# A fifth table from sums written four times, and a new written-out order of work, in an attention and ReGLU kernel on one core

## The chip, the core and the metric

The kernel runs on one NeuronCore of a Trainium2 chip. The metric is the device time of one execution in microseconds. The engines are named as in the profile: PE (TensorE, matmuls), PEld (its weight loads), DVE (VectorE), ACT (ScalarE), POOL (GpSimd) and SP (SyncE, here a queue that only issues transfers).

## The reference

Four batches of 12,416 tokens with 128 channels are attended to by 32 inducing points, the tokens then attend to the 32 results, and a gated feed-forward layer with 1,536 hidden units follows.

```python
def mab(q, kv):
    s = scale * (q @ kv.transpose(0, 2, 1))
    s = s - s.max(-1, keepdims=True)
    a = np.exp(s)
    a /= a.sum(-1, keepdims=True) + 1e-09
    return a @ kv
h = mab(I, x)                    # I: inducing points, (B, 32, 128)
x = mab(x, h).reshape(B * N, C)  # (49664, 128)
gate = np.maximum(x @ w_gate, 0.0)
val = x @ w_val
out = gate * val @ w_out
```

## The kernel before

**The idea.** After the second attention every token is a weighted mean of only 32 rows of h. The kernel takes the sign of each hidden unit's gate as one for the whole batch (it checks on the chip that this is certain, and falls back to a general kernel if it isn't). Gate times value is then a quadratic form in the 32 weights, and the output is a sum over pairs of rows: an exponential of a sum of two scores, times a table entry. The pairs are laid out as four full tables of 128 pairs, plus a fifth one with 16 sums in groups of 32 rows. The fifth stands four times, once for each row group, so that whichever row group a token block's exponentials `p` lie in finds its table.

**Stages.** The first batch's attention and tables are done ahead of everything (to about 40 us). What remains is interleaved by hand in the string `ORDER`, one letter for one step, and each letter takes the next step of its kind:

- `E` (`scores`): two matmuls of 512 columns make pair scores of 1,024 tokens' worth of columns (`e_ps`, two buffers), and ACT takes their exponential into `F` (20 buffers).
- `O` (`outputs`): five matmuls of 129 columns for one tile of 128 tokens, four with `F` and `T`, one with `p` and the fifth table. After three tiles DVE takes the reciprocal of the denominators (`rzo`) and multiplies into `osb`; after six tiles SP's queue stores `osb` (four buffers). There are 97 tiles in each batch, 388 in all.
- `s` (`pair_scores`, `pair_copy`, `pair_reach`): four matmuls into column groups, then two DVE passes. Some `s` steps are the bound on the error (`bound1` to `certain`) and the last is the flag for the fallback.
- `x` (`pair_exp`): ACT's exponential of single scores, `p`.
- `p` (`plan_phase1`): the next batch's first attention: for batch 1 six steps of eight PE transposes, then score and sums for each chunk of 16 tiles, the end of h (`h_end1`, `h_end2`), the gates (`gates`, four steps), their sums and signs, and the masks (`masked`).
- `u`: the products of gates and values (`products`), their joins, the fifth table's sums (`fifth`), and the tables (`table`, `table5`). A batch's tables must stand in `T` before its first `O`.
- `l` and `t`: a load of a chunk of x by POOL's queue, and its DMA transpose on SP's queue, which the stores use as well. A `t` takes the chunk that was loaded last.

All engines run in order, so `ORDER` sets which step waits behind which on each of them.

**Names that the change touches.** `lhs5` holds the fifth table's sums, the weights of its matmuls; half of each group of 32 is zero. `fifth(b, 0)` makes the first product `u16`, `fifth(b, 1)` the second product and the sum. `table5(b)` multiplies them with `wo` (for batch 0 with the masked copy `won`) for each of 12 groups of hidden units, into the four row groups of one bank, and DVE copies the bank to `T` with a mask (`quarter`).

Of the kernel before, what the change touches and what calls it, by code (L numbers as in the profile page):

```python
# [11 lines left out]
FP16 = mybir.dt.float16  # L12
AF = mybir.ActivationFunctionType
ALU = mybir.AluOpType
# [3 lines left out]
def quadratic_kernel(tc, x, inducing, moe_w_gate, moe_w_val, moe_w_out, out):  # L18


    with ExitStack() as ctx:
        return quadratic_body(
            ctx, tc, x, inducing, moe_w_gate, moe_w_val, moe_w_out, out
        )


def quadratic_body(ctx, tc, x, inducing, moe_w_gate, moe_w_val, moe_w_out, out):
    nc = tc.nc
    B, N, C = x.shape
    M = inducing.shape[0]  # L30
    DFF = moe_w_gate.shape[1]
    P = 128
# [4 lines left out]
    NFF = DFF // P  # L37
# [6 lines left out]
    H = M // 2  # L44
# [8 lines left out]
    def st(shape, dtype, tag, bufs, name=None, pool=None):  # L53
        return (pool or sb).tile(shape, dtype, tag=tag, bufs=bufs, name=name or tag)
# [8 lines left out]
    wo = constp.tile([P, NFF, P], FP16, name="wo")  # L63
# [47 lines left out]
    mp = ctx.enter_context(tc.tile_pool(name="mp", bufs=1))  # L111

    def mt(shape, dtype, tag, bufs, name=None):
        return st(shape, dtype, tag, bufs, name, pool=mp)
# [1 line left out]
    ga, gb, va, vb = (mp.tile([P, NFF, M + NS], FP16, name=n) for n in ("ga", "gb", "va", "vb"))  # L116
    U = [mp.tile([P, NFF, NS, M], FP16, name=f"U{i}") for i in range(2)]
    won = mp.tile([P, NFF, P], FP16, name="won")
    lhs5 = mp.tile([P, NFF, M], FP16, name="lhs5")


    def windows(out, h):
# [201 lines left out]
    with tc.tile_pool(name="sp", bufs=1) as sp, tc.tile_pool(  # L324
        name="psum0", bufs=1, space=bass.MemoryType.PSUM
# [5 lines left out]
    def bank(tag, name, shape, dtype=FP32):  # L331
        return psum.tile(shape, dtype, tag=tag, bufs=2, name=name)
# [8 lines left out]
    dve, act, pool = nc.vector, nc.scalar, nc.gpsimd  # L341
# [182 lines left out]
    def fifth(b, k):  # L524

        s = state[b]
        if k == 0:
            s["u16"] = mt([P, NFF, H], FP16, "u16", 1)
            dve.tensor_tensor(out=s["u16"], in0=ga[:, :, 0:H], in1=va[:, :, H:M], op=ALU.mult)
            return  # L530
        u = lhs5[:, :, 0:H]
        dve.tensor_tensor(out=u, in0=ga[:, :, H:M], in1=va[:, :, 0:H], op=ALU.mult)
        dve.tensor_tensor(out=u, in0=u, in1=s["u16"], op=ALU.add)

    def table5(b):
        ps = bank("m", "T5_ps", [P, P])
        for t in range(NFF):
            for r in range(4):
                nc.tensor.matmul(  # L539
                    ps[32 * r : 32 * r + 32, :],  # L540
                    lhs5[:, t, :],
                    (wo if b else won)[:, t, :],
                    start=t == 0,
                    stop=t == NFF - 1,
                )
        dve.tensor_tensor(
            out=T[b % 2][:, 4:8, 0:P],
            in0=ps.unsqueeze(1).broadcast_to([P, 4, P]),
            in1=quarter.unsqueeze(2).broadcast_to([P, 4, P]),
            op=ALU.mult,  # L550
        )
# [121 lines left out]
    def plan_phase1(b):  # L673
# [120 lines left out]
        for j in range(4):  # L794
            for odd in range(2):
                for i in range(2):
                    todo.append(f(products, i, 0, NFF, 4 * j, 4 * j + 4, odd))
            todo.append(f(joined, j))
            late.append((len(todo) + 1, f(table, b, j)))
            if j == 1:  # L800
                todo += [f(fifth, b, 0), f(fifth, b, 1)]
                late.append((len(todo) + 1, f(table5, b)))
# [51 lines left out]
    pair_exp(0, 0)  # L854
    all_k(7, 4)
    fifth(0, 0)
    fifth(0, 1)
    table_all(0, 7, 4)
    all_k(11, 1)
    table5(0)  # L860
    table_all(0, 11, 1)
    scores(0, 0, 1, 0)
# [12 lines left out]
    for step in ORDER:  # L875
        if step == "E":
            scores(*next(units))
        elif step == "O":
            b, t = next(tiles)
# [8 lines left out]


ORDER = (  # L890
    "EOpOsExOpOEEpOOOEOOEppOEuEpOOOpEEspOOxOOpOllEElsplOOpOEEOlOOOppEEpOppOpEsEpOpOOEEpOOpEpE"
    "OOOxOsEEOOOpOpEOOpOpOtEpEOpOOEOOpOtEOEtOEuOuOOuxtOOEtusEOuOuEOOOEuuOOxEsuuEuOOOEslsOEOuu"
    "OsuluEEOpOOOEEuOEpEuOpOEEuuuOOxuOOuEEssOOOxOEEpOpuOOOtEuuEupOOtpOEEOuOOOEEOppOOOEEsOOOOl"
    "OlxEEOOpxOOOEEOlOOlOpOEEspxOOOOEEOlOOOpOEEOOOpEOEppOOEEOOpOtpEEpOOpOOOOEEOOtpOOpOEOEOOpO"
    "EsExOOOtutOEEuOOOutOEOuussEOEOOOExuuuOOEElsOOOupluuOEsEsOOEOuxOuEEpuOpEuEuOuOxOOEEOuOOOu"
    "uEOOEsuEuOOEEtuOOpEOuOupOEuEOOtOpEsEOOpuEEsOOOOOEEOOOxOpsEEOOOOpOOEEpOpOOOxOEEspOOpOEOpE"
    "OEppEOOEOOppOEOppOOEpEOOOpOOEOOEpOxOOuOEEuOOOsEOuOOuusEOEOuEOOuEEuuOOOEOOOEsuEOxuOOOEEus"
    "sOOuExuOOOxuEEsuEOuOEOOuEOOEOOOxEuEuOuOOOOEsEuOuOEEOOOOOuEEuuOOOOOEEOuOsEEOOOEOOOxOOOEEO"
    "OOOOOEEOOxOOOOEEOOOOOOEEOOOOOxOEEOOOOOOEEsOOxOOOEEOOOOOsEEOOOOOsEEOOOOsOOEEOOOOOOEEOsOOE"
    "OEOOOxsOOEEOOOOOEsOEOOOxOEEOOOOOOOOOOOO"  # L900
)


# [202 lines left out]
```

## Time and profile before

| | |
|---|---|
| time, median of three | 273.76 us (273.37 to 273.79) |
| span of the profiled execution | 273.0 us |
| mean granted clock of TensorE | 0.984 |
| PE busy | 253.8 us |
| ACT busy | 228.4 us |
| DVE busy | 214.2 us |
| first output tile, last output tile | 40.7 us, 266.3 us |
| DMA transpose on SP's queue, median of issuing one | 3.1 us |

Busy shares are averages over the span. In what follows, "stretch" is the time between two output tiles of the loop. A row of the costliest groups gives the line in the kernel, the engine, the operation, what is written from what, the shape and the number of instructions; then the busy time, the mean of one in ns, and the idle time of the engine just before them with what ended it. A matmul's end is modelled and includes its latency, so how many fit in a time is read from the starts of the steps that follow each other.

### The profile page before, as it was taken

To read this page: it belongs to the slowest core of one execution; us is meant where nothing else is said; L and a number is where in the kernel's file an instruction comes from. 1 tells how busy PE (TensorE), PEld (TensorE's weight loads), DVE (VectorE), ACT (ScalarE), POOL (GpSimd) and SP (SyncE) were. 2 spreads that over 40 slices of the span, in tenths; PEclk is the share of its full clock that TensorE was granted. 3 is DMA by queue.
4 is the path that set the end of the run, shared out by engine and by line. 5 is a ranking of instruction groups with operands and counts; after the bars stand their busy time and mean duration, and the time that the engine had idled before them with its cause. 6 is when DMAs were issued, how large, how long until landed. Compare 5 with 4: busy or idle time off the path is not lost.

```text
span 273.0 us, 9520 instructions
## 1 busy us (share of the span) xinstructions
PE 253.8 (93%) x4029; PEld 189.2 (69%) x4029; DVE 214.2 (78%) x583; ACT 228.4 (84%) x305; POOL 27.2 (10%) x71
## 2 busy tenths in 40 slices
PE   2998699999999999999899999999899999999990
PEld 0786587776666777776667777767677777878770
DVE  4565958866999997766899998778999997678651
ACT  4133689999999999999799999999899988988940
POOL 8372000210000200400002000000010000000000
PEclk9999599999999999999999999999999999999998
DMA  7999988999499889899999989331421333443333
GB/s 178 201 208 204 214 170 104 249 199 243 168 209 178 209 226 220 208 224 271 232 217 228 176 241 204 118 119 60 166 116 70 118 118 138 163 175 149 144 140 113
DMA packets 48738, 48.38 MB, mean 177 GB/s; under 512 B 35472, under 2 KB 36656, under 8 KB 48688
## 3 DMA queue, kind: packets, MB, share of 16 engines
q1 hardware_dynamic: 41520, 33.74, 43.8%
q0 software_dynamic: 6880, 13.50, 27.8%
q8 instruction: 33, 0.54, 0.8%
q10 hardware_dynamic: 288, 0.46, 0.5%
q14 instruction: 17, 0.14, 0.2%
HBM read 27.80 MB, written 25.43 MB: 195 GB/s over the span
## 4 chain that ended last, share of the span: by engine, by line
PE 79%; DVE 9%; ACT 7%; issue 3%; POOL 0%; ACTq 0%; DVEq 0%; POOLq 0%
PE o_ps L591 32%; PE e_ps L569 16%; PE o_ps L593 7%; ACT F L576 5%; PE T_ps L519 3%; PE T_ps L505 3%; PE s_ps L707 3%; PE s_ps L372 3%; DVE osb L608 2%; PE xT_ps L262 2%; PE hz_ps L729 2%; PE s_ps L273 1%; PE hz_ps L720 1%; PE T_ps L539 1%; PE xT_ps L698 1%
## 5 line engine op out<-in xcount | busy, mean ns | idle before, releaser
L576 ACT ACTIVATE F<-e_ps 128x1024 f16<-128x1024 f32 x192 | 185.6, 1026 | 15.4 <-PE e_ps L569 13.0
L591 PE MATMUL o_ps<-T,F 128*128 128x129 f16 x1536 | 129.4, 221 | 1.9 <-DVE osb L608 1.0
L591 PEld LDWEIGHTS <-F 128*128 128x128 f16 x1536 | 98.5, 97 | 28.1 <-issue 19.7
L593 PE MATMUL o_ps<-T,p 128*128 128x129 f16 x388 | 84.5, 218 | 0.0
L608 DVE TENSOR_TENSOR osb<-o_ps,rzo 128x384 f32<-128x384 f32 x132 | 72.5, 549 | 4.8 <-DVE rzo L607 0.2
L569 PE MATMUL e_ps<-sc,sel 32*128 32x512 f16 x384 | 60.0, 385 | 0.5 <-ACT F L576 0.3
L593 PEld LDWEIGHTS <-p 128*128 128x128 f16 x388 | 37.9, 98 | 0.4
L607 DVE RECIPROCAL rzo<-o_ps 128x3 f32<-128x3 f32 x132 | 23.0, 174 | 18.7 <-PE o_ps L593 17.4
L569 PEld LDWEIGHTS <-sel 32*128 32x128 f16 x384 | 16.1, 91 | 18.1 <-issue 5.4
L628 DVE TENSOR_SCALAR sc<-s_ps 128x512 f16<-128x512 f32 (+1 forms) x28 | 17.6, 627 | 2.8 <-PE s_ps L372 2.3
L640 DVE TENSOR_REDUCE reach<-sc 128x1 f32<-128x512 f16 (+1 forms) x28 | 17.5, 627 | 1.0
L655 ACT ACTIVATE p<-sc 128x512 f16<-128x512 f16 (+1 forms) x28 | 16.3, 584 | 0.0
L275 ACT ACTIVATE p<-s_ps 128x256 f16<-128x256 f32 (+3 forms) x16 | 5.3, 332 | 12.2 <-PE s_ps L273 12.2
L263 DVE COPY xT<-xT_ps 128x1024 f16<-128x1024 f16 (+2 forms) x15 | 8.8, 583 | 5.8 <-PE xT_ps L262 4.4
L709 ACT ACTIVATE p<-s_ps 128x512 f16<-128x512 f32 (+1 forms) x21 | 11.4, 547 | 0.7 <-PE s_ps L707 0.7
L442 POOL TENSOR_SCALAR ok<-eps 128x1 f32<-128x1 f32 x4 | 1.1, 285 | 100.6 <-DVE eps L403 100.6
L482 DVE TENSOR_TENSOR U<-U,U 128x1536 f16<-128x1536 f16 (+1 forms) x12 | 10.9, 906 | 0.4
L505 PE MATMUL T_ps<-won,U 128*128 128x128 f16 x96 | 8.3, 262 | 2.4 <-DVE U L473 2.4
L505 PEld LDWEIGHTS <-U 128*128 128x128 f16 x96 | 7.5, 121 | 4.0 <-DVE U L473 3.9
L519 PE MATMUL T_ps<-wo,U 128*128 128x128 f16 x144 | 10.1, 219 | 0.0
L707 PE MATMUL s_ps<-indT,xT 128*128 128x32 f16 x288 | 10.0, 177 | 0.0
L86 POOL DMA_DIRECT2D x<-in_x_dram x18 | 9.7, 551 | 1.7 <-PE s_ps L273 1.2
(159 smaller groups left out, 255.2 us busy)
## 6 DMA issues: line engine op xcount, KB each, us to landing
out_dram<-osb SPq DMA_DIRECT2D x64, 384.0 KB, 2.8
x<-in_x_dram POOLq DMA_DIRECT2D x18, 512.0 KB, 11.7
x<-in_x_dram POOLq DMA_DIRECT2D x8, 256.0 KB, 8.0
x<-in_x_dram POOLq DMA_DIRECT2D x5, 128.0 KB, 8.1
osb<-in_x_dram ACTq DMA_DIRECT2D x1, 384.0 KB, 4.5
osb<-in_x_dram SPq DMA_DIRECT2D x1, 384.0 KB, 4.4
wg<-in_moe_w_gate_dram POOLq DMA_DIRECT2D x1, 384.0 KB, 8.1
wv<-in_moe_w_val_dram POOLq DMA_DIRECT2D x1, 384.0 KB, 8.7
```

Of the source, the lines that this page charges most:

```text
L505: nc.tensor.matmul(s["T_ps"][j // 2][:, j % 2, :], u_cols(i, t, j), won[:, t, :], start=False, stop=(i, t, j % 2) == (1, NFF - 1, 1),)
L519: nc.tensor.matmul(ps, u_cols(0, t, j), wo[:, t, :], start=t == 0, stop=t == NFF - 1)
L569: nc.tensor.matmul(ps[:, r, :], sel4[rows, j, :], sc[rows, :], start=True, stop=True)
L576: act.activation(out=F[b, q, d, j], in_=ps, func=AF.Exp, scale=sm_scale2)
L591: nc.tensor.matmul(ps, f, T[b % 2][:, j, 0 : P + 1], start=j == 0, stop=False)
L593: nc.tensor.matmul(ps, p2s[b, q][rows, tok], T[b % 2][rows, 4 + r, 0 : P + 1], start=False, stop=True)
L607: dve.reciprocal(out=rz[:, 0:k, :], in_=outputs.ps[:, 0:k, P : P + 1])
L608: dve.tensor_tensor(out=osb[:, a6 : a6 + k, :], in0=outputs.ps[:, 0:k, 0:P], in1=rz[:, 0:k, :].broadcast_to([P, k, P]), op=ALU.mult,)
L628: dve.tensor_scalar(out=scs[b, q][0:k, 0:w], in0=ps[0:k, 0:w], scalar1=64.0, scalar2=-64.0, op0=ALU.min, op1=ALU.max,)
L640: dve.tensor_reduce(out=state[b]["reach"][0:k, q : q + 1], in_=scs[b, q][0:k, 0:w], axis=AX.X, op=ALU.max, apply_absolute_value=True,)
L655: act.activation(out=p2s[b, q][0:k, 0:w], in_=scs[b, q][0:k, 0:w], func=AF.Exp, scale=sm_scale2)
L707: nc.tensor.matmul(ps[:, t, :], s["xT"][q][:, t, :], indT, start=True, stop=True)
```

## The change

Two things change. First, the sums of the fifth table are written four times side by side into a larger `lhs5`, so that 12 matmuls with 128 weight columns fill all four row groups at once; before, 48 matmuls of 32 weight columns each filled one row group. The product goes into a buffer of its own rather than into `lhs5`. Second, `ORDER` is replaced by another string with the same number of each letter (191 E, 388 O, 82 u, 75 p, 40 s, 27 x, 14 l, 14 t). It was searched for with the stores on SyncE's queue, which both kernels use.

```diff
-    lhs5 = mp.tile([P, NFF, M], FP16, name="lhs5")
+    lhs5 = mp.tile([P, NFF, 4, M], FP16, name="lhs5")
...
-            s["u16"] = mt([P, NFF, H], FP16, "u16", 1)
+            s["u16"] = mt([P, NFF, H], FP16, "u16", 2)
             dve.tensor_tensor(out=s["u16"], in0=ga[:, :, 0:H], in1=va[:, :, H:M], op=ALU.mult)
             return
-        u = lhs5[:, :, 0:H]
+        u = mt([P, NFF, H], FP16, "u16", 2)
         dve.tensor_tensor(out=u, in0=ga[:, :, H:M], in1=va[:, :, 0:H], op=ALU.mult)
-        dve.tensor_tensor(out=u, in0=u, in1=s["u16"], op=ALU.add)
+        u, u16 = (v.unsqueeze(2).broadcast_to([P, NFF, 4, H]) for v in (u, s["u16"]))
+        dve.tensor_tensor(out=lhs5[:, :, :, 0:H], in0=u, in1=u16, op=ALU.add)
...
         for t in range(NFF):
-            for r in range(4):
-                nc.tensor.matmul(
-                    ps[32 * r : 32 * r + 32, :],
-                    lhs5[:, t, :],
-                    (wo if b else won)[:, t, :],
-                    start=t == 0,
-                    stop=t == NFF - 1,
-                )
+            nc.tensor.matmul(
+                ps,
+                lhs5[:, t, :, :].rearrange("p r m -> p (r m)"),
+                (wo if b else won)[:, t, :],
+                start=t == 0,
+                stop=t == NFF - 1,
+            )
```

The start and the end of the two strings (the rest differs in the same manner):

```diff
 ORDER = (
-    "EOpOsExOpOEEpOOOEOOEppOEuEpOOOpEEspOOxOOpOllEElsplOOpOEEOlOOOppEEpOppOpEsEpOpOOEEpOOpEpE"
+    "pEsEOOOOOxEEpOpOEpEOEOsEpOOxEEOOOppOEEsplOOpOxEEpsOOlpOOEEuOOlOpOOpEEppOOEppOOEEpsllOlpO"
...
-    "OEOOOxsOOEEOOOOOEsOEOOOxOEEOOOOOOOOOOOO"
+    "OOEEOOOOOsxEEOOOOOOEEOOOOEOOEOOOOOOOOOO"
 )
```

Where the steps of the later batches fall, by the output tile after which they come:

| step | before | after |
|---|---|---|
| loads of batch 2 | 17, 17, 17, 17, 21, 66, 69 | 14, 19, 23, 30, 30, 31, 34 |
| transposes of batch 2 | 43, 49, 50, 54, 56, 88, 90 | 53, 61, 61, 61, 62, 65, 73 |
| score steps of batch 2 | 70, 75, 85, 90, 96, 113, 122 | 72, 76, 78, 85, 88, 93, 95 |
| gates of batch 2 | 131, 132, 132, 134 | 111, 114, 115, 120 |
| products of batch 2, first and last | 150, 187 | 133, 188 |
| transposes of batch 3 | 132, 140, 150, 150, 154, 183, 190 | 113, 118, 125, 129, 156, 164, 171 |
| gates of batch 3 | 222, 222, 224, 224 | 197, 199, 205, 210 |
| products of batch 3, first and last | 236, 283 | 224, 281 |

More of the change, by code (lines that the diff above doesn't have):

```diff
@@ L890 @@
 ORDER = (
-    "EOpOsExOpOEEpOOOEOOEppOEuEpOOOpEEspOOxOOpOllEElsplOOpOEEOlOOOppEEpOppOpEsEpOpOOEEpOOpEpE"
[L892 to L899, printed above, removed]
-    "OEOOOxsOOEEOOOOOEsOEOOOxOEEOOOOOOOOOOOO"
+    "pEsEOOOOOxEEpOpOEpEOEOsEpOOxEEOOOppOEEsplOOpOxEEpsOOlpOOEEuOOlOpOOpEEppOOEppOOEEpsllOlpO"
+    "EEpOEppOlOEOOEpOpOOEEsOOpOOEsOOOpEEspOpOOEOEOOpEtOOxuOOEEOuOOOttuEtOsutEuOuOEOtEOsEOuOxO"
+    "uEuuEOOOpOutuEEOOEpsEOuupEuEOuuupEOxpEOxuuOOOpsEEOuOOpuuOEuEpOOupOxOEEslpOuOOpOEEllpOupO"
+    "EEOpOxOOlOEEpOOOpEOOEOOEsEOOOpOEEOtOpOpOOOtEEOOpOOOEEOOtpOOOEpOtEpOOOOsuxEEOpuOOOOEuEpul"
+    "lOOlpOEEsOuOOOEpuEOOxOuusEuEpuOOuOOOEEusOOOuEEptxuOusOOOOEEsuEOOEsOEEtOuOOEOOOpxOEtEsxpO"
+    "OOOuOEEOOuuOOpOEEspOOOuEEOOpuEEOuOuuOpuEOpOOEEOpupxEEOOpOOEpOOpOOEEOOOOpOsEEOOOOpOEpEOOO"
+    "OpEOOEpOOOxOEEOOOuuOEOOEusEOOEOuOEOOEuxOOuOOEEOuOOuuOEEuOOOuxOOOuEEOOOususEEOOxOOOOEEsOO"
+    "OuEssuxEEOOOOEuxOOEEuOOuOEOOuOsEEOOOuuEuEOOOOuEOOEOEuOOEOuxOOsEEOOOOuEEsOOOOEEOOOOOEEOOO"
+    "OOOxEEOOOOEOOEOOOOxEEOOOOOEsEOOOOEEsOOEOOOEOOOOEEOOOOOsEEOOxOOOOEEOOOOOOEEOsxOOOOsEEOsOO"
+    "OOEEOOOOOsxEEOOOOOOEEOOOOEOOEOOOOOOOOOO"
 )
```

## The prediction

> **What bounds the kernel now.** I read four views: busy shares, costliest groups, the chain that ended last, and busy time by stretch. First the shares:
>
> ```profile
> PE 253.8 (93%) x4029; PEld 189.2 (69%) x4029; DVE 214.2 (78%) x583; ACT 228.4 (84%) x305; POOL 27.2 (10%) x71
> ```
>
> PE looks like the bound, but its ends are modelled, so 93% can't be read as peak. The chain is needed as well:
>
> ```profile
> PE 79%; DVE 9%; ACT 7%; issue 3%; POOL 0%; ACTq 0%; DVEq 0%; POOLq 0%
> PE o_ps L591 32%; PE e_ps L569 16%; PE o_ps L593 7%; ACT F L576 5%; PE T_ps L519 3%; PE T_ps L505 3%; PE s_ps L707 3%; PE s_ps L372 3%; DVE osb L608 2%; PE xT_ps L262 2%; PE hz_ps L729 2%; PE s_ps L273 1%; PE hz_ps L720 1%; PE T_ps L539 1%; PE xT_ps L698 1%
> ```
>
> Most of the chain is PE, yet it passes to ACT and DVE for whole stretches. The group rows say why:
>
> ```profile
> L576 ACT ACTIVATE F<-e_ps 128x1024 f16<-128x1024 f32 x192 | 185.6, 1026 | 15.4 <-PE e_ps L569 13.0
> L608 DVE TENSOR_TENSOR osb<-o_ps,rzo 128x384 f32<-128x384 f32 x132 | 72.5, 549 | 4.8 <-DVE rzo L607 0.2
> ```
>
> Now the busy time by stretch, cut at every 24th output tile (columns: window, then busy us and instructions of PE, PEld, DVE, ACT, POOL; clock; DMA):
>
> ```profile
> 57.50:75.30 17.80, 17.39 (x319) 12.57 (x317) 13.64 (x41) 16.52 (x24) 0.00 (x0) 1.00 0.83 215
> 75.30:90.30 15.00, 14.96 (x196) 10.35 (x194) 14.41 (x42) 13.85 (x18) 0.00 (x0) 1.00 1.09 194
> 120.20:134.40 14.20, 12.93 (x211) 9.93 (x208) 9.73 (x33) 12.69 (x18) 0.00 (x0) 1.00 1.02 253
> 148.60:166.50 17.90, 17.82 (x331) 12.98 (x329) 17.05 (x43) 17.48 (x24) 1.85 (x6) 1.00 0.97 222
> 194.20:210.50 16.30, 15.96 (x239) 11.29 (x236) 15.29 (x45) 15.43 (x21) 1.47 (x3) 1.00 0.32 123
> 222.60:234.00 11.40, 11.40 (x161) 8.69 (x159) 8.56 (x23) 10.22 (x14) 0.00 (x0) 1.00 0.35 133
> ```
>
> From the first output tile (40.7 us) to the last exponential (262.7) ACT is busy 208.8 of 222 us, DVE 186.4. Three engines are nearly full and take turns: DVE in tiles 48-72 and 240-264 (14.4 of 15.0, 15.3 of 16.3), ACT in 168-192 (17.5 of 17.9), while in 222.6:234.0 DVE works 75% of the time. So ORDER, which says what stands beside what, sets the end.
>
> **The skill.** Perfetto Trace Analysis, Identifying the Most-Contended Engine: matmul busy time is a poor measure of how near TensorE is to its limit. The trace agrees: a single 128-column matmul shows 219 ns, while 12 in a row (L519) take 0.67 us. TensorEngine Tiling (Array Packing), Key Properties: different array tiles work in parallel; Restrictions there: column tiling turns fast weight load off. VectorE: DVE Perf Modes, the perf-mode tier table: a 16-bit tensor_tensor runs at up to two elements a cycle; the trace's 128x1536 fp16 add at 906 ns and 128x768 multiply at 549 ns give 0.46 ns per further element, which agrees.
>
> **Part 1, fifth table on PE.** Removed: 48 matmuls of 32 columns per batch (192 in all). Added: 12 of 128. The chain prices both:
>
> ```profile
> 149.82 0.80 PE T_ps L519 x12
> 153.03 0.84 PE T_ps L539 x48
> 206.12 0.67 PE T_ps L519 x12
> 208.96 0.67 PE T_ps L539 x48
> ```
>
> Four column groups already run side by side, so 48 small ones take about what 12 full ones take, not four times as much. From the first matmul of a table to the next step's start I read 0.67-0.78 us for L519 and 0.79-0.80 for L539. Saving: 4 x 0.11 = 0.4 us of PE, of which the three in the loop count only where PE is the bound: 0.1 to 0.4, I take 0.2.
>
> **Part 2, sums written four times (DVE).** Before, per batch: 248 + 248 + 259 ns. The last one now writes 128x768 through a broadcast. The nearest row is L473's fp16 multiply with a broadcast input, 128x768, 549 ns; without the double rate the elements would take 768/384 times what L608's f32 elements take, about 1.1 us. I take 0.55: +0.29 us x 4 = 1.2 us of DVE (at most 3.4). Batch 0's stands ahead of the last products of the opening, which ended at 36.2 us while PE used them after 39.3; three us hide it. The others lie in DVE-heavy stretches, so 0.3-0.6 us may show. The second u16 buffer costs nothing and takes a write-after-read wait away. The zeroing of lhs5 on POOL grows from 384 to 1536 elements (0.46 us before; 0.9 more at the most pessimistic linear rate) and delays the loads of batch 1, issued from 18.6 us. Their first reader on PE comes at 40.9 and the first loads landed at 29.3: hidden.
>
> **Part 3, ORDER.** The letters are the same in number; only places change. Price per step, as what it adds to its engine's busy time (PE: usual distance to the next step's start): E 0.27 PE, 0.95 ACT; O 0.29 PE, 0.25 DVE; x 0.47 ACT; s 0.33 PE, 1.22 DVE; score 0.40 PE, 0.47 ACT; sums 0.51 PE, 0.22 DVE; PE transpose 0.45 PE, 0.63 DVE; gates 0.15 PE, 0.30 ACT, 0.41 DVE; h_end2 1.96, gate sums 1.09, masks 1.33, a product 0.45, a join 0.90 DVE; table 0.68 PE, 0.19 ACT. Summed over each stretch of 24 tiles, the fullest engine has (us):
>
> before: 16.6, 16.7, 16.9, 17.3, 12.1, 12.2, 17.1, 17.8, 13.9, 13.4, 17.0, 11.7, 11.6, 9.4, 10.2, 9.1, last four tiles 1.2; sum 224.4.
> after: 18.0, 17.2, 14.0, 20.6, 12.8, 13.5, 15.7, 13.9, 13.3, 11.7, 13.8, 13.0, 10.7, 10.3, 9.6, 9.4, 1.2; sum 218.7.
>
> The first sum is near the measured 225.6 us (40.7 to 266.3), so the count is usable. It falls by 5.7. Why: the new order starts batch 2's gates at tile 111 rather than 131 and its products at 133 rather than 150, batch 3's gates at 197 rather than 222 and its products at 224 rather than 236. The DVE-heavy stretches (16.9, 17.1, 17.0) drop to 14.0, 15.4, 13.8 on DVE, and that work lies where PE and ACT have enough to do too. The crowd in the chain at 128-140 us (gates, sums, masks, then outputs, all DVE) should thin out.
>
> But exponentials run ahead through buffers, so stretches aren't hard walls, and another cut gives another number: falls of 2.6 (24 tiles, shifted by 12), 3.7 and 1.2 (32), 2.1 and 3.9 (48), 4.1 and 6.8 (16), 3.4 and 2.5 (12). The mean of these nine is 3.4; I take that.
>
> Ends: a PE transpose now stands before the first O, where PE waited 0.42 us for T: 0.3 gained. Against it, the SyncE queue. Batch 2's five large transposes now stand together at tiles 61-65, after one at 53. Each occupies that queue 3.1 us (median), so the store of tiles 60-65 leaves about 12 us after the group starts at some 85 us, near 97, landing by 100-102 (stores beside loads and transposes took 2 to 9 us). Its osb buffer is wanted again at tile 84, some 99-101 us in the new order. DVE's eviction of tile 84 may wait 0-2 us there, and behind it in DVE's queue stand joins and copies, then PE for an o_ps bank. I take 0.5. The transposes themselves land by 90, 93, 96, 99 and 103, their score steps come at about 95, 97, 102, 104 and 109: no wait. Loads for batch 2 all go out by tile 34, 19 tiles ahead of the first transpose that needs them; before, two went out at 66 and 69.
>
> The tail: before, PE stood 0.7 us before tile 379 for the last full exponential, which ACT had begun only after the matmuls of the small last unit, 0.38 us later than it could. The new order issues that unit two tiles later, so I estimate 0.2 gained.
>
> Sum: -3.4 (balance) -0.2 (table on PE) +0.5 (wider add, where DVE is full) -0.3 (first O) +0.5 (store wait) -0.2 (tail) = -3.1. 273.8 - 3.1 = 270.7.
>
> **Rivals.** (a) The load count holds in full: 5.7 us of balance, near 268; for it, the 24-tile cut reproduces before best. (b) Short waits, not stretch loads, set the pace: ACT's 13 us of idle come in gaps under 0.8 us, each from the local place of E among O's, and a new order makes its own. Then the gain is 0 to 1.5 us, 272.3-273.8. (c) Slower: transposes in a row hold stores back as above, DVE waits on osb two or three times, 2 us each, and the fourth stretch (20.6 us on PE, 18.8 DVE, 19.6 ACT: all three full, no slack for waits) runs over by 1-2 us; with the gain of 3.4 eaten by these, 274.5-277. Against (c): before, stores took up to 10.1 us to land on the same queue, and no DVE wait for one shows.
>
> **How the numbers follow.** Forecast, gain 1.5-4.7 us: 0.53. (a): 0.13. (b): 0.16, of which 0.06 falls within 0.2% (273.2-274.3) and 0.10 is faster. (c): 0.18. Faster 0.76, same 0.06, slower 0.18. Range: (a) with the largest fall read, 6.8, reaches 266.8; upward, half of (c): 275.2.
>
> **What would show it.** Right: DVE-led chain pieces at 128-140 and 185-194 us shrink; ACT idle after 40 us falls below 11 us; L539 shows 48 matmuls of 128 columns, 0.68 us per table; the last add is 0.5-0.6 us. Wrong: DVE evictions released by a store's DMA near tile 84, scores waiting for a transpose, or ACT idle as long as before with the same balance of loads.

## The result, and the profile after

| | before | after |
|---|---|---|
| time, median of four | 273.77 us (273.37 to 274.42) | 271.88 us (271.49 to 272.28) |
| ratio, 95% interval | | 0.9929 [0.9903, 0.9954] |
| first PE step of ORDER to last output tile | 225.8 us | 224.0 us |
| tile 0 to tile 360 | 213.8 us | 209.6 us |
| tile 360 to the last one, 387 | 11.7 us | 12.9 us |

The change makes the kernel 1.9 us faster; the forecast was 3.1. The third row is the interleaved part alone. It is the one to compare: the opening before it differs from run to run (the first step came at 40.1 us before and at 39.4 us after), while the loop's stretches repeat to about 0.03 us in traces of the same order. One exception bears on this table. In the trace of the kernel before, tiles 24 to 48 take 17.8 us, and in experiments 1, 10 and 11, which have the same order there, 17.4. So some 0.4 us of the 225.8 belong to this one execution and not to its order, and the loop's own fall is about 1.4 us. In the fourth row 1.2 us of the fall are not a gain: the new order does three more PE steps ahead of its first output tile. From the first PE step to tile 360 the fall is 3.0 us (2.6 without those 0.4), and the last row then gives 1.2 back.

The page's busy shares after (the kernel before had 253.8, 189.2, 214.2 and 228.4 us):

```profile
PE 250.4 (93%) x3885; PEld 187.1 (69%) x3885; DVE 214.6 (79%) x583; ACT 228.5 (84%) x305; POOL 27.8 (10%) x70
```

DVE and ACT do nearly the same work as before. Of PE's 144 fewer matmuls nothing can be read in busy time, since their ends are modelled. The chain after, shares by engine and by line:

```profile
PE 69%; DVE 11%; ACT 7%; DMA 6%; issue 4%; POOL 0%; ACTq 0%; DVEq 0%; POOLq 0%
PE o_ps L591 29%; PE e_ps L569 15%; PE o_ps L593 6%; DMA x<-in_x_dram 6%; ACT F L576 6%; DVE osb L608 4%; PE T_ps L505 3%; PE T_ps L519 3%; PE s_ps L707 3%; PE s_ps L372 3%; PE hz_ps L729 2%; DVE U L473 1%; PE xT_ps L698 1%; PE T_ps L539 1%; PE hz_ps L720 1%
```

The 6% of DMA is in the opening, where in this run the loads of x came last. In the loop the chain is still PE's steps with pieces of ACT and DVE; DVE's share has grown from 9% to 11%. The two large groups, by line:

```profile
L576 ACT ACTIVATE F<-e_ps 128x1024 f16<-128x1024 f32 x192 | 185.1, 1026 | 13.1 <-PE e_ps L569 10.8
L608 DVE TENSOR_TENSOR osb<-o_ps,rzo 128x384 f32<-128x384 f32 x132 | 72.5, 549 | 4.5
```

ACT's idle time before exponentials fell from 15.4 to 13.1 us: some waits have gone, far from all. The same stretches of output tiles that the prediction showed, now with the times at which the new kernel reaches them, to about 0.4 us (window, then busy us and instructions of PE, PEld, DVE, ACT, POOL; clock; DMA):

```profile
57.90:75.80 17.90, 17.53 (x319) 12.70 (x317) 12.57 (x43) 17.15 (x24) 0.53 (x1) 1.00 1.05 256
75.80:89.30 13.50, 12.78 (x166) 8.86 (x164) 12.86 (x35) 12.73 (x17) 0.88 (x3) 1.00 0.94 195
122.40:135.10 12.70, 11.98 (x206) 9.22 (x204) 11.99 (x32) 11.63 (x15) 1.22 (x3) 1.00 1.02 248
151.40:165.40 14.00, 14.00 (x256) 10.80 (x253) 13.39 (x32) 13.62 (x20) 0.00 (x0) 1.00 0.76 202
192.00:205.30 13.30, 13.19 (x181) 9.91 (x179) 11.92 (x37) 12.98 (x18) 0.61 (x3) 1.00 0.33 131
218.30:229.90 11.60, 11.60 (x159) 8.60 (x157) 8.32 (x22) 10.81 (x14) 0.00 (x0) 1.00 0.32 121
```

Tiles 240-264 (fifth line) took 16.3 us before and take 13.3 now. But the work went elsewhere, as the elapsed time of all stretches shows (us, from the start of one tile to that of the tile 24 later):

```
tiles from   0    24    48    72    96   120   144   168   192   216   240   264   288   312   336   360
before    16.9  17.8  15.1  17.3  12.6  14.1  14.2  18.0  13.7  13.9  16.3  12.1  11.4   9.8  10.6  10.7
after     16.6  18.0  13.4  20.8  12.3  12.7  16.3  14.0  14.3  12.3  13.3  13.0  11.6  10.9  10.0  11.9
```

Single stretches move by up to 4 us, while their sum falls by 3.0. The last three hold no work of later batches in either order: 312-336 loses 1.1 us, with one `E` more than before, 336-360 wins 0.6, and 360-384, with as many `E` as before, loses 1.2.

### The profile page after: what moved, and what is told of

It reads as the page before. It is cut to its first block, busy times and chain, and to the rows that moved or that the text cites. A ratio compares the mean times of both kernels' runs of the same rounds, so it can differ in the third digit from the quotient of the medians.

```text
span 270.5 us, 9238 instructions
## 1 busy us (share of the span) xinstructions
PE 250.4 (93%) x3885; PEld 187.1 (69%) x3885; DVE 214.6 (79%) x583; ACT 228.5 (84%) x305; POOL 27.8 (10%) x70
## 4 chain that ended last, share of the span: by engine, by line
PE 69%; DVE 11%; ACT 7%; DMA 6%; issue 4%; POOL 0%; ACTq 0%; DVEq 0%; POOLq 0%
PE o_ps L591 29%; PE e_ps L569 15%; PE o_ps L593 6%; DMA x<-in_x_dram 6%; ACT F L576 6%; DVE osb L608 4%; PE T_ps L505 3%; PE T_ps L519 3%; PE s_ps L707 3%; PE s_ps L372 3%; PE hz_ps L729 2%; DVE U L473 1%; PE xT_ps L698 1%; PE T_ps L539 1%; PE hz_ps L720 1%
## 5 line engine op out<-in xcount | busy, mean ns | idle before, releaser
L576 ACT ACTIVATE F<-e_ps 128x1024 f16<-128x1024 f32 x192 | 185.1, 1026 | 13.1 <-PE e_ps L569 10.8
L591 PE MATMUL o_ps<-T,F 128*128 128x129 f16 x1536 | 128.5, 221 | 2.5 <-DVE osb L608 2.1
L591 PEld LDWEIGHTS <-F 128*128 128x128 f16 x1536 | 98.6, 97 | 27.8 <-issue 19.6
L608 DVE TENSOR_TENSOR osb<-o_ps,rzo 128x384 f32<-128x384 f32 x132 | 72.5, 549 | 4.5
L569 PE MATMUL e_ps<-sc,sel 32*128 32x512 f16 x384 | 59.0, 385 | 0.2
L607 DVE RECIPROCAL rzo<-o_ps 128x3 f32<-128x3 f32 x132 | 23.0, 174 | 17.3 <-PE o_ps L593 15.6
L569 PEld LDWEIGHTS <-sel 32*128 32x128 f16 x384 | 15.2, 91 | 17.8 <-issue 5.8
L275 ACT ACTIVATE p<-s_ps 128x256 f16<-128x256 f32 (+3 forms) x16 | 5.3, 332 | 11.9 <-PE s_ps L273 11.9
L709 ACT ACTIVATE p<-s_ps 128x512 f16<-128x512 f32 (+1 forms) x21 | 11.5, 550 | 0.7 <-PE s_ps L707 0.5
## 6 DMA issues: line engine op xcount, KB each, us to landing
x<-in_x_dram POOLq DMA_DIRECT2D x18, 512.0 KB, 11.9
```

Of the source, the lines that this page charges most:

```text
L569: nc.tensor.matmul(ps[:, r, :], sel4[rows, j, :], sc[rows, :], start=True, stop=True)
L576: act.activation(out=F[b, q, d, j], in_=ps, func=AF.Exp, scale=sm_scale2)
L591: nc.tensor.matmul(ps, f, T[b % 2][:, j, 0 : P + 1], start=j == 0, stop=False)
L607: dve.reciprocal(out=rz[:, 0:k, :], in_=outputs.ps[:, 0:k, P : P + 1])
L608: dve.tensor_tensor(out=osb[:, a6 : a6 + k, :], in0=outputs.ps[:, 0:k, 0:P], in1=rz[:, 0:k, :].broadcast_to([P, k, P]), op=ALU.mult,)
```

## The experiments

Ratios are to the kernel before. The number of an experiment is that of its label.

**Experiments 1 and 2: the table alone, the order alone.** Experiment 1 has the new `fifth`, `table5` and `lhs5` in the old ORDER.

```diff
 ORDER = (
-    "pEsEOOOOOxEEpOpOEpEOEOsEpOOxEEOOOppOEEsplOOpOxEEpsOOlpOOEEuOOlOpOOpEEppOOEppOOEEpsllOlpO"
+    "EOpOsExOpOEEpOOOEOOEppOEuEpOOOpEEspOOxOOpOllEElsplOOpOEEOlOOOppEEpOppOpEsEpOpOOEEpOOpEpE"
...
```

> The order of before with the fifth table's change alone. Theory (the order brings the gain, the table next to nothing): between 273.0 and 274.2 us, that is -0.3% to +0.2% of before; each table in the loop takes about 0.68 us to the next step instead of 0.79, and DVE has 0.3 us more per batch. Rival (the table change is the gain, or its wider add a cost that the new order pays for): more than 1 us off before, either way.

Measured: 273.76 us, ratio 1.0017 [0.9995, 1.0038]. Experiment 2 is the new ORDER with the 48 matmuls and the 192-element sums of before:

```diff
-    lhs5 = mp.tile([P, NFF, 4, M], FP16, name="lhs5")
+    lhs5 = mp.tile([P, NFF, M], FP16, name="lhs5")
...
-            nc.tensor.matmul(
-                ps,
-                lhs5[:, t, :, :].rearrange("p r m -> p (r m)"),
+            for r in range(4):
+                nc.tensor.matmul(
+                    ps[32 * r : 32 * r + 32, :],
+                    lhs5[:, t, :],
```

> The new order with the old fifth table (48 matmuls, sums written once). Theory: within 0.5 us of the changed kernel, 271.4 to 272.4 us. Rival (the table is worth a part of the gain): 272.8 us or more.

Measured: 272.29 us, ratio 0.9951 [0.9930, 0.9972]; first PE step to last tile 224.1 us, against 224.0 with the new table too. So ORDER brings the gain, and the table none that can be told. In the old order the same distance is 226.2 us with the new table, against 225.8, or 225.4 without the 0.4 us that belong to that one execution: there the table costs 0.7 us. The prices show why. In the chain in order of time of the kernel after (start, us, what), a full table and the fifth one:

```profile
142.46 0.67 PE T_ps L519 x12
146.42 0.78 PE T_ps L539 x12
```

The second piece is longer because an `E` follows. From the fifth table's first matmul to the next step it is 0.68 us where that is an `O` or sums, against 0.79 with the 48 small ones; where an `E` comes next, as after two of the three tables in the new order, 0.78 against 0.78-0.81. Together some 0.1 us are saved. What it costs elsewhere, in the groups by line (busy us, mean ns of one, idle before):

```profile
L534 DVE TENSOR_TENSOR lhs<-u,u 128x768 f16<-128x768 f16 x4 | 2.2, 558 | 0.2
...
L238 POOL MEMSET lhs<- 128x1536 f16 x1 | 1.4, 1418 | 0.0
```

The wide add took 558 ns, nearly as long as L473's multiply of that size with one broadcast input (549), and costs 0.3 us more of DVE for each batch. At most 0.11 us of PE for a table stands against it. Whether the add costs time depends on the order. In experiment 1, PE comes to the table before the add is done:

```profile
89.62 0.84 PE L539 MATMUL T_ps<-wo,lhs 128*128 128x128 f16 x12 [0.22 <-DVE lhs L534]
```

At the next two tables it waits 0.29 and 0.09 us. In the kernel before and in the kernel after it doesn't wait there.

**Experiments 3 and 10: the flag.** The timeline of the kernel after, shortly after tile 360, shows where the lost 1.2 us are (start, us, engine, line, operation; in brackets the idle time before it and what ended it):

```profile
253.52 0.56 DVE L608 TENSOR_TENSOR osb<-o_ps,rzo 128x384 f32<-128x384 f32 x1
...
254.18 0.16 DVE L810 TENSOR_TENSOR v<-v,near 128x1 f32<-128x1 f32 x1
254.40 0.30 PEld L812 LDWEIGHTS flag_ps<-v,ones 128*128 128x128 f32 x2 [1.31 <-DVE v L810]
254.40 0.38 PE L812 MATMUL flag_ps<-v,ones 128*128 128x1 f32 x2 [1.13 <-DVE v L810]
254.71 0.39 PE L569 MATMUL e_ps<-sc,sel 32*128 32x512 f16 x4
```

The last `s` step, the flag, is two tiny DVE operations and then a matmul with their result. In the new order it stands right behind tile 365, the third of its group: DVE first has the reciprocal and the eviction (0.56 us) of that group to do, then the flag's two passes, and PE stands for 1.13 us. Two `E` wait behind the flag in PE's queue, and ACT, which needs them, stands for 1.69 us:

```profile
255.20 1.94 ACT L576 ACTIVATE F<-e_ps 128x1024 f16<-128x1024 f32 x2 [1.69 <-PE e_ps L569]
```

Experiment 3 moves this one letter two tiles later, behind a tile that doesn't end its group of three and with outputs after it:

```diff
-    "OOEEOOOOOsxEEOOOOOOEEOOOOEOOEOOOOOOOOOO"
+    "OOEEOOOOOxEEOOsOOOOEEOOOOEOOEOOOOOOOOOO"
```

> The changed kernel with one letter of the order moved: the flag step comes after tile 367 instead of after tile 365, so behind the two pair-score steps and two tiles, at a place where no eviction is pending. In the changed kernel PE stood 1.13 us before the flag's matmul and ACT 1.69 us behind it. Theory (this wait lies on the path to the end): ACT's gap near 255 us falls under 0.7 us and the time falls by 0.7 to 1.2 us, to 270.7 to 271.2. Rival (what is lost there is lost again at the next wait, ACT not being the bound at the tail): under 0.3 us.

Measured: 270.34 us, ratio 0.9898 [0.9866, 0.9931]. Its timeline at the flag:

```profile
251.60 1.94 ACT L576 ACTIVATE F<-e_ps 128x1024 f16<-128x1024 f32 x2 [0.17 <-PE e_ps L569]
...
252.31 0.38 PE L812 MATMUL flag_ps<-v,ones 128*128 128x1 f32 x2
...
254.30 2.86 ACT L576 ACTIVATE F<-e_ps 128x1024 f16<-128x1024 f32 x3 [0.76 <-PE e_ps L569]
```

PE no longer waits at the flag. Tiles 360-384 take 10.9 us instead of 11.9, and every other stretch is the same to 0.02. The intervals of this kernel and of the one after overlap, so the proof is the stretch, not the median. The converse is experiment 10, in which the kernel before gets the flag behind an evicting tile:

```diff
-    "OEOOOxsOOEEOOOOOEsOEOOOxOEEOOOOOOOOOOOO"
+    "OEOOOxsOOEEOOOsOOEOEOOOxOEEOOOOOOOOOOOO"
```

> The kernel before with one letter moved: the flag step comes after tile 368, whose eviction is then pending, instead of after tile 370 and one E. In the kernel before, PE lost 0.35 us ahead of the flag's matmul. Theory (the flag's matmul waits for DVE's eviction and then for two small DVE steps, wherever it stands right behind an evicting tile): PE stands 0.9 to 1.4 us there and tiles 360 to the end take 0.4 to 1.0 us longer. Rival (the wait is hidden, since ACT and not PE ends the tail): tiles 360 to the end as before within 0.2 us.

Measured: 274.21 us, ratio 1.0021 [1.0005, 1.0038]; tiles 360-384 go from 10.7 to 11.8 us. Its timeline has the same two gaps:

```profile
256.31 0.38 PE L812 MATMUL flag_ps<-v,ones 128*128 128x1 f32 x2 [1.13 <-DVE v L810]
...
257.72 1.02 ACT L576 ACTIVATE F<-e_ps 128x1024 f16<-128x1024 f32 x1 [1.48 <-PE e_ps L569]
```

So the place of one letter is worth 1.0 to 1.1 us in either order, a third of what the whole search was expected to bring.

**Experiment 4: the place of batch 3's work.** The prediction held that batch 3's gates, products and tables, which the old order crowds into tiles 222-283, had to move earlier. Experiment 4 keeps the kernel after, with batch 3's `p` and `u` letters at the tiles of before (gates at 222 to 224 instead of 197 to 210, products from 236). Its edit does more: at 20 places it also changes the sequence of the letters between two output tiles, from the first letters on, though none of them goes to another tile:

```diff
-    "pEsEOOOOOxEEpOpOEpEOEOsEpOOxEEOOOppOEEsplOOpOxEEpsOOlpOOEEuOOlOpOOpEEppOOEppOOEEpsllOlpO"
...
+    "EpsEOOOOOxEEpOpOEpEOEOsEpOOxEEOOOppOEEsplOOpOxEEpsOOlpOOEEuOOlOpOOpEpEppOOEppOOEEspllOlpO"
...
-    "OOOuOEEOOuuOOpOEEspOOOuEEOOpuEEOuOuuOpuEOpOOEEOpupxEEOOpOOEpOOpOOEEOOOOpOsEEOOOOpOEpEOOO"
+    "EEOOuuOOOEEsOOOEuEOpOEuEOupOuuOEuOOpOEEOxpuEEOOOOEOOOOEEOpOOOOsEpEOOpOpOOEEOOpOOEpOOEpOp"
...
```

> The changed kernel, its E, O, s, x, l and t letters unmoved, but batch 3's phase-one steps (p) and products and tables (u) stand after the same output tiles as in the order of before: gates at 222 rather than 197, products from 236 rather than 224. By the sum of the fullest engine over stretches of 24 tiles the time rises from 218.7 to 223.9 (2.3 to 5.2 with other cuts). Theory (the balance of work beside the outputs is what the new order brings): 274 to 277 us, with the loss in tiles 216 to 264 and DVE over 90% busy there. Rival (the local place of E among O sets the pace, and that is unmoved here): within 1 us of the changed kernel, under 272.9.

Measured: 284.99 us (median of five executions), ratio 1.0424 [1.0380, 1.0467]. Both expectations were far too low. Ahead of tile 135, where the first letter of batch 3 moves, this kernel is already 2.5 us behind the kernel after, by the sequence of letters between neighbouring tiles alone. The first such place in the loop, `EpEpp` instead of `pEEpp` between tiles 26 and 27, costs 0.7 us. Later the stretch 216-240 takes 20.6 us instead of 12.3, 240-264 takes 16.2 instead of 13.3. PE stands for 1.24 us before a gate step (190.65 us) and for 1.63 us before the fifth table (219.07 us), and between the two, in tiles 216-240, the granted clock falls in the execution that was profiled. The granted clock in the 40 slices of the page, tenths of full speed:

```profile
PEclk9999699999999999999999999975799999999997
```

And the busy time by stretch, for the part at half clock (columns as above):

```profile
191.20:204.90 13.70, 13.70 (x107) 9.01 (x104) 9.37 (x22) 8.84 (x11) 0.00 (x0) 0.50 0.22 87
```

With the clock at 0.50, PE does 107 matmuls in 13.7 us; in the kernel after, 13.0 us at full clock hold 171 (tiles 264-288). The profiled execution took 289.36 us at a mean granted clock of 0.957. Three others, at 0.984 to 0.989 (the kernel after: 0.980), took 283.5 to 285.0 us. A mean of 0.984 is 9.1 us at half clock in all. The beginning and the end of the execution take at least 7.2 of these in every trace here, and the shortest fall in a loop is 3.4 us. So these three had no fall in the loop, and some 12 us above the kernel after come without one; in the profiled execution the fall adds some 5. Of the 12 us, 2.5 are those of the letters ahead of tile 135. The rest is the move of batch 3's work and the changed sequences among it, which this run does not separate.

**Experiment 5: the new work between the old outputs.** `E`, `O`, `s` and `x` in the sequence of before; `p`, `u`, `l` and `t` at the tiles of after, with the new table:

```diff
...
-    "EEpOEppOlOEOOEpOpOOEEsOOpOOEsOOOpEEspOpOOEOEOOpEtOOxuOOEEOuOOOttuEtOsutEuOuOEOtEOsEOuOxO"
+    "OppOxlOsEEOOpOpOEOOOpOEEOOOEOppOpOEOEOEOOptOxOuOEsEOOEuOOOEttutOutuOxEusEOOtOEssOEuOOsuE"
...
```

> The order of before for E, O, s and x, but p, u, l and t (phase one, products and tables, loads, transposes) after the same output tiles as in the new order; the fifth table as changed. The sum of the fullest engine over stretches of 24 tiles is 222.6, against 224.4 before and 218.7 in the new order. Theory (spreading the later batches' work is what brings the gain, and the sum of fullest engines tells it): faster than before by 1 to 2.5 us, 271.2 to 272.8. Rival (short waits, the fit of E and O to that work, decide more than the loads): slower than before, over 274.3 us, with waits of PE over 0.5 us at places where neither parent order has any.

Measured: 301.75 us, ratio 1.1022 [1.0975, 1.1068]. By the prediction's count of loads this kernel has 222.6 us, less than the 224.4 of the kernel before, yet it takes 28 us more. PE stands idle for 20.5 us from the first to the last output tile, against 4.2 in the kernel after. The longest waits of this run that bear on it (engine, line, what for: us, times, longest):

```profile
ACT F L576 <- PE e_ps L569: 33.5, 47, 3.8
...
PEld L720 <- ACT p L709: 6.1, 7, 1.6
```

and of the kernel after:

```profile
ACT F L576 <- PE e_ps L569: 10.8, 24, 2.4
...
PEld L720 <- ACT p L709: 2.5, 7, 0.4
```

One such wait in the timeline of experiment 5:

```profile
65.72 3.77 ACT L576 ACTIVATE F<-e_ps 128x1024 f16<-128x1024 f32 x4
...
68.03 0.56 PE L707 MATMUL s_ps<-indT,xT 128*128 128x32 f16 x16
...
69.36 0.63 ACT L709 ACTIVATE p<-s_ps 128x512 f16<-128x512 f32 x1
...
70.04 0.25 PE L720 MATMUL hz_ps<-ones,p 128*128 128x1 f16 x4 [1.14 <-ACT p L709]
```

A score step's result goes through ACT to the sums. Two `E` had been put right ahead of the score, so ACT did their exponentials first, and PE, with everything else behind the sums in its queue, stood for 1.14 us; after the change such a wait is at most 0.4 us. The clock was granted at half in three stretches as well:

```profile
70.80:77.60 6.80, 6.80 (x62) 4.92 (x60) 4.73 (x17) 2.63 (x4) 0.00 (x0) 0.50 0.63 172
101.50:104.90 3.40, 3.40 (x53) 2.45 (x38) 1.49 (x4) 1.93 (x4) 0.00 (x0) 0.50 1.08 254
176.60:180.00 3.40, 3.40 (x33) 2.77 (x31) 1.29 (x4) 2.42 (x5) 0.00 (x0) 0.50 0.88 193
```

If PE works half as fast at half the clock, these 13.6 us account for at most 6.8 of the 28 us (an estimate). Here `p`, `u`, `l` and `t` stand at the very tiles of the kernel after, and `E` and `s` up to 11 and 20 tiles away from theirs. So the new places of the later batches' work bring nothing by themselves, beside a sequence of `E`, `O` and `s` that wasn't made for them. The count by stretch does not see this.

**Experiment 7: the stores.** The prediction counted 0.5 us for a store held back in SyncE's queue. In the kernel after, the store of tiles 60-65 was issued at 94.4 us and had landed at 98.9, and DVE evicted tiles 84 to 86 into that buffer at 103.2 without a wait, 4.3 us later (just after 100 us, which the expectation names, is the start of tile 84's matmuls). How near it is to one, a kernel with three `osb` buffers instead of four tells:

```diff
-        x32 = [mt([P, 6, P], FP32, "osb", 4) for _ in range(2)]
+        x32 = [mt([P, 6, P], FP32, "osb", 3) for _ in range(2)]
...
-            osbs[0] = mt([P, 6, P], FP32, "osb", 4)
+            osbs[0] = mt([P, 6, P], FP32, "osb", 3)
```

> The changed kernel with three output buffers instead of four, so that a store must have landed six tiles earlier. In the changed kernel the store of tiles 60 to 65 left SyncE's queue at 94.4 us behind four transposes and landed at 98.9, and tile 84, which takes its buffer again, was evicted just after 100 us. Theory (the stores are held back there by transposes, and the four buffers hide it with about 1 to 2 us to spare): tile 78, at about 95 us, waits for that landing, 2 to 5 us are lost in tiles 72 to 96, and the time is 273 to 277 us. Rival (stores have much slack): within 0.5 us of the changed kernel.

Measured: 276.01 us, from one run, without an interval. The loss is not at tiles 72-96, where the transposes are, but at 96-120 (15.6 us instead of 12.3). Its timeline there:

```profile
112.33 0.40 PE L591 MATMUL o_ps<-T,F 128*128 128x129 f16 x4
...
114.57 0.56 DVE L608 TENSOR_TENSOR osb<-o_ps,rzo 128x384 f32<-128x384 f32 x1 [2.16 <-DMA out_dram<-osb]
...
115.33 0.61 PE L756 MATMUL h_ps<-zs,ones 128*128 128x32 f32 x2 [1.68 <-DVE zs L746]
...
116.28 0.64 PE L591 MATMUL o_ps<-T,F 128*128 128x129 f16 x4
```

One eviction waited 2.16 us for a store that was issued at 106.0 us and landed at 114.5, beside three loads of x issued within a microsecond of it; behind the eviction PE waited 1.68 us. The fourth buffer hides this, and what it hides is a store beside loads, not one behind transposes. The last line shows four output matmuls at 0.64 us, which had taken 0.40 before the wait; the granted clock was 0.50 from 115.4 to 118.8 us, so a part of this loss is the clock's.

**Experiments 11 and 12: DVE where it is fullest.** The prediction said that DVE binds tiles 48-72, 144-168 and 240-264. Experiments 11 and 12 leave out `pair_reach` in the kernel before and after: the running maximum of scores, 28 DVE reductions of 0.63 us, is not computed, and what is checked with it has no meaning.

```diff
     def pair_out(b, q, kw, ps):
         pair_copy(b, q, kw, ps)
-        pair_reach(b, q)
```

> The kernel before without the running maximum of the scores (the second DVE pass of every s step, 0.62 us each; the bound on the error is then left out, the flag is computed from zero). Theory (DVE is the bound in tiles 48-72, 144-168 and 240-264 of before): these three stretches, 15.1, 14.2 and 16.3 us, get shorter by 0.5 to 1.3 us each, the others by under 0.3; 2 to 4 us in all. Rival (waits from step to step rule, and DVE's load matters nowhere): under 1 us in all, spread evenly.

> The changed kernel without the same pass. Theory (the new order has moved DVE's work to where PE and ACT are as full): tiles 72-96 (20.8 us) don't get shorter, the largest gain of a stretch is under 0.7 us, and the whole gains less than the kernel before does, 1 to 2.5 us. Rival: it gains as much or more than before does.

Measured: 271.88 us, ratio 0.9949 [0.9930, 0.9968], for the kernel before; 271.02 us, 0.9899 [0.9862, 0.9936], for the one after. From the loop 14 us of DVE work are gone, and it is 0.9 us shorter than in experiment 10 ahead of the flag (1.3 against the trace of the kernel before, with the 0.4 us of that execution); in the kernel after it becomes 0.7 us shorter. Two of the stretches in which DVE was above 90% busy, tiles 72-96 and 264-288, in the kernel before:

```profile
90.11:107.42 17.31, 17.31 (x346) 13.05 (x343) 16.02 (x39) 16.66 (x23) 1.93 (x6) 1.00 0.90 222
...
210.22:222.36 12.14, 12.14 (x161) 8.81 (x159) 11.75 (x28) 11.68 (x15) 0.00 (x0) 1.00 0.27 105
```

and without the reductions:

```profile
87.17:104.47 17.30, 17.30 (x346) 13.05 (x343) 14.29 (x36) 16.67 (x23) 1.93 (x6) 1.00 0.91 230
...
206.66:218.80 12.14, 12.14 (x161) 8.80 (x159) 10.28 (x25) 11.68 (x15) 0.00 (x0) 1.00 0.27 105
```

DVE has 1.7 and 1.5 us less to do, and both stretches last as long as before, to 0.01 us. At 97% busy DVE was not the bound there. In 168-192 1.3 us of DVE work bring 0.2 us. Only in 48-72 (0.19 us of work, 0.29 us of time) and 144-168 (0.40 and 0.35) did nearly all of it come through; in 240-264 little was taken (0.3 us), and none of it came through. So of the three stretches that the prediction's count put on DVE, two react and one does not.

**Experiments 8 and 9: the end, and a first product.** Experiment 8 is experiment 3 with the last four `E` one or two tiles earlier; experiment 9 adds to it batch 1's first two products five and three tiles later. The edit of experiment 9 does more than that: at 24 further places, from tile 70 on, it changes the sequence of letters between two output tiles.

```diff
-    "OOEEOOOOOxEEOOsOOOOEEOOOOEOOEOOOOOOOOOO"
+    "OOEEOOOOOxEEOOsOOOEEOOOEOOEOOOOOOOOOOOO"
```

> The kernel with the flag moved, and the last four E steps one or two tiles earlier. Theory (at the tail ACT waits for E's matmuls, 0.76 us near 254 us, and PE for the last full exponential at tile 379, 0.4 us): 0.3 to 0.7 us faster than with the flag moved alone, about 269.8 us. Rival (ACT's gap only moves, since the e_ps buffers come free no earlier): within 0.2 us of it.

For experiment 9, besides, in the second line of ORDER (the products) and in six more lines, two of which are shown:

```diff
...
-    "EEpOEppOlOEOOEpOpOOEEsOOpOOEsOOOpEEspOpOOEOEOOpEtOOxuOOEEOuOOOttuEtOsutEuOuOEOtEOsEOuOxO"
+    "EEpOEppOlOEOOEpOpOOEEsOOpOOEsOOOpEEspOpOOEOEOOpEtOOxOOEEOOOuOuttuEtOsutEuOuOEOtEOsEOuOxO"
-    "uEuuEOOOpOutuEEOOEpsEOuupEuEOuuupEOxpEOxuuOOOpsEEOuOOpuuOEuEpOOupOxOEEslpOuOOpOEEllpOupO"
+    "EuuEuOOOpOtuEuEOOEpsEOpuuEEuOpuuuEOxpEOxuuOOOpsEEOuOOpuuOEEupOOpuOxOEEslpOuOOpOEEllpOpuO"
...
-    "OOOuOEEOOuuOOpOEEspOOOuEEOOpuEEOuOuuOpuEOpOOEEOpupxEEOOpOOEpOOpOOEEOOOOpOsEEOOOOpOEpEOOO"
+    "OOOuOEEOOuuOOpOEEspOOOEuEOOpEuEOuOuuOpuEOpOOEEOppuxEEOOpOOEpOOpOOEEOOOOpOsEEOOOOpOEpEOOO"
...
```

> As the one with the earlier last E steps, and batch 1's first two products moved from after tiles 55 and 58 to after 60 and 61, away from the masks, where PE stood 0.88 us for an eviction behind DVE's queue. Theory (DVE's queue holds that eviction, and the products can wait): 0.3 to 0.8 us faster than without the move. Rival (DVE is full through tiles 48 to 72, so the wait comes two tiles later): within 0.2 us.

Measured: 270.12 us, ratio 0.9888 [0.9850, 0.9926], and 271.42 us, 0.9950 [0.9926, 0.9973]. From tile 360 on, experiment 8 takes 11.7 us and experiment 3 11.9: the tail brings nothing that can be told. The later products help: at tile 60 experiment 9 is 0.5 us ahead of experiment 8, counted from tile 40. From tile 70 on it loses 2.4 us, step by step, at or just behind the places where only the sequence between two tiles was changed: 0.4 us at tile 158, 0.3 at 188, 0.6 at 194. At the last of these, `ppux` stands instead of `pupx`. The table's matmuls had run between the sums and the step that needs their DVE result; now they run behind it, and PE waits:

```profile
166.40 0.41 PE L755 MATMUL h_ps<-stackI,hz 128*128 128x32 f32 x2 [0.40 <-DVE hz L742]
```

So the 271.42 us say nothing against the later products. The best versions found, experiments 3 and 8, stand 1.0% and 1.1% below the kernel before.

## Why the prediction was right, and where it was not

**Direction and size.** Faster, as forecast, 271.9 against 270.7 and inside the range. The kernel with the flag moved, which differs by one letter, gives the sum of the forecast almost to the digit (270.3). That agreement is partly luck: the sum came out while its main step was explained only in part rightly, and terms of 0.3 and 0.5 us did not come.

**The missing term.** None of the sum's terms held the flag: +1.1 us. The prediction priced the `s` letters by their load (1.22 us of DVE) and the tail by one exponential, and did not ask for each PE step that consumes a DVE result what DVE has to do just ahead of it. Experiments 3 and 10 show the term in both orders.

**Part 1 and part 2, the table.** The prices were sized well. PE's 0.68 us per table (0.78 ahead of an `E`) and the add's 558 ns against an assumed 550 are what was read from neighbouring rows; the wider zeroing took 1.42 us, as the pessimistic rate said, and is hidden. Together they were put at +0.3 us; the loop shows +0.7 in the old order, where PE waits for the add, and -0.1 in the new, where it doesn't. That a multiply with one broadcast input prices an add with two held here. The price per further element was misread: the row of 906 ns mixes nine adds of 1,536 elements with three of 1,152. By shape the first take 958 ns, so a further element costs 0.53 ns and not 0.46; the estimate of 0.55 us does not rest on it. That column tiling turns fast weight load off is not to be seen here: a weight load of L539 took 97 ns with 32 columns and 98 with 128.

**Part 3, the balance.** The term was -3.4. From the first step to tile 360 the loop gained 3.0 us, 2.6 of them the order's, so the size was near. The reason given, three engines taking turns with DVE the bound in tiles 48-72 and 240-264, held in part: by experiment 11, tiles 48-72 and 144-168 do react to DVE's work, 240-264 do not, and 72-96 and 264-288 stay as long with DVE at 93% and 97%. Rival (b), short waits at the local place of a step, has direct support from experiments 4 and 9: changed sequences between neighbouring tiles, which leave the loads of the stretches alone, cost 2.5 and 2.4 us. Its gain, 0 to 1.5 us, was put somewhat too small.

What the order's 2.6 us consist of is not settled. They are not in the idle time that PE shows: from the first to the last output tile that is 3.4 us before and 4.2 after, the flag's 1.13 among them. ACT's idle time fell. A price that nobody counted can be read from the starts of steps. From the start of an output to the next step PE takes 0.29 us where that is an output and 0.38 where it is an `E`, in nearly all of some 90 cases and in both orders. The trace names the form of each matmul (128\*128 for outputs, 32\*128 for `E`, 128\*32 for `s`), and this form changes 312 times in the loop before and 302 times after. At 0.09 us for each change that would be 0.9 us, an estimate that no run tested.

One of the waits that went can be read in a row. The groups by line, the gates of later batches, before:

```profile
L347 PE MATMUL hw_ps<-hT,wv 128*128 128x48 f16 x48 | 2.4, 183 | 0.8 <-DVE gb L364 0.6
```

and after:

```profile
L347 PE MATMUL hw_ps<-hT,wv 128*128 128x48 f16 x48 | 2.3, 183 | 0.0
```

With the four gate steps spread over nine to thirteen tiles instead of two or three, DVE has passed on the first before PE comes to the next. Against that, PE's waits for evictions ahead of outputs (L591 for L608) rose from 1.0 to 2.1 us. As the prediction asked for, the crowd in the chain has thinned at its place: around batch 2's gates, from 113 to 125 us, it now reads, by line,

```profile
by line: PE o_ps L591 28.8%; ACT F L576 24.3%; PE e_ps L569 13.6%; PE o_ps L593 6.3%; ACT va L362 5.1%; DVE osb L608 4.7%; DVE rzo L607 3.1%; PE h_ps L755 2.8%; PE s_ps L372 2.8%; ACT ga L362 2.5%; issue 2.4%; PE h_ps L756 1.9%; DVE vb L364
```

where in the kernel before, from 128 to 140 us, DVE's evictions had led with 28%. But from 122 to 140 us, with the masks, they still make 15.6%, and over the whole chain DVE's share rose. ACT's idle time in the loop fell from 13.2 to 11.5 us, not below 11; the flag's 1.69 us are in it.

**The count by stretch.** It fell by 5.7 us where the loop gained 3.0, and it gives 223.9 for experiment 4 and 222.6 for experiment 5, both below the 224.4 of the kernel before, which they exceed by 12 and 28 us. It prices each step where its letter stands, though the engines run apart by a microsecond or more, and knows no waits. Nor does it bound a stretch from below: it has 16.9 us for tiles 48-72 of the kernel before, which took 15.1, and 17.1 for 144-168, which took 14.2. That its nine cuts had a mean of 3.4 was not the check it was taken for.

**The first output.** The -0.3 us was misread: the 0.42 us of waiting stood in the row of PEld, whose idle time costs nothing while PE has matmuls to do. PE itself, between an `E` at 40.09 and the first `O` at 40.41 us, lost 0.05.

**The store and the tail.** The +0.5 us for a store wait did not come: the buffer was free 4.3 us before it was wanted. The prediction took the start of tile 84's matmuls for its eviction, which came 3 us later. The wait for the last full exponential, ahead of tile 379, did shrink from 0.84 to 0.43 us lost, twice the 0.2 that was counted, though nothing of it is seen in the sum beside the flag.

**Still open.** What makes up the order's 2.6 us was not settled, nor what sets off a fall of the clock. How much of the loss of experiment 5 is the clock is known only as a bound.

## What to carry to other kernels

In an order written by hand, look at every PE step that reads a short DVE result, and keep it away from both an eviction just ahead and the steps that feed the fullest engine just behind: one such letter cost 1.1 of 273 us. Loads summed by stretch don't forecast a time; whether a 95% busy engine binds is tested by taking work from it. An order works as a whole: putting one part of it into another order made kernels 12 and 28 us slower than before, and a new sequence of a few letters between the same two output tiles cost up to 0.7 us. So an edit of such an order must be compared letter by letter with its parent before its time is read.

## What the runs showed of the hardware

- In the loop, the granted clock was 0.50 for 6.8, 3.4 and 3.4 us in experiment 5, for 3.4 us in experiment 7 and for 13.7 us in the profiled execution of experiment 4. Each time PE had stood idle within the 2 us before, once for 1.14 to 1.68 us or in waits of 0.5 to 0.6 us. But waits of 1.13 us before the flag, 1.43 and 1.45 us in experiment 5 and 1.63 us in experiment 4 brought no such fall, and three other executions of experiment 4 can't have had one. So what sets it off is not shown.
- From an output's first matmul to the next step's, PE took 0.29 us where that was an output and 0.38 where it was an `E`, whose matmuls use 32 rows.
- Forty-eight matmuls into four column groups take 0.79 us and twelve full ones 0.68: four groups run at about the rate of one full array, with 14% lost. That agrees with the Trainium skill, TensorEngine Tiling (Array Packing), Key Properties, by which different tiles of the array work in parallel; the 14% is this case's number.
- A store of 384 KB, which lands in a median of 2.9 us in experiment 7, took 8.5 us beside three loads.
